# Weight 0 in two parts, the output weight in two halves, and one cast moved to GpSimd

## The chip, the cores and the metric

The kernel runs on one core of a Trainium2 chip. The core has a matrix engine (TensorE, PE in the profile, with its weight loads shown apart as PEld), a vector engine (VectorE, DVE), a scalar engine (ScalarE, ACT), a general engine (GpSimd, POOL) and an engine that mostly issues transfers (SyncE, SP). Transfers between the chip's memory and the core run on 16 DMA engines. Here SP issues the loads of q, k and v, and POOL issues the loads of the weights, which are turned from float32 into bfloat16 on the way. The metric is the time of one execution on the device in microseconds (us), lower is better.

## The reference

Attention with a sliding window of 128 positions and 4 sink positions, over 4 batches, 8 heads, 768 positions and 64 elements a head; then a feed-forward layer that takes the maximum of three products.

```python
scores = scale * q @ k.T                     # per batch and head, 768 x 768
keep   = (key < 4) | ((0 <= query - key) & (query - key < 128))
a      = softmax(where(keep, scores, -1e9))
x      = (a @ v)  -> [3072, 512]             # the 8 heads side by side
h      = max(x @ w1, x @ w2, x @ w3)         # each w is [512, 768]
out    = h @ w_out                           # w_out is [768, 512]
```

The text calls w1, w2 and w3 weight 0, 1 and 2, and w_out the output weight.

## The kernel before

The 3072 positions are cut into 12 chunks of 256 positions, three to a batch. A chunk is loaded as q, k and v of all 8 heads (512 KB each in float32), cast to bfloat16, and q and k are transposed so that the head's elements lie along the partitions. For each of four pairs of heads `score` multiplies keys and queries on PE, `expo` takes the exponential on ACT, `mask` or a mask added beforehand by `premask` cuts the window, `av` multiplies with v on PE, and DVE divides by the sum (a reciprocal and a multiplication, L353 and L356) and writes x. `xpose` transposes x on PE. Then `ffn_h(chunk, third, weight)` multiplies x with 256 of the 768 columns of one weight (eight matmuls, L388); the result for weight 0 is copied by ACT, those for weights 1 and 2 are merged by DVE with a maximum. `ffn_y(chunk, half)` multiplies h with the output weight, six matmuls, one for each block of 128 rows of it (L409).

Nothing reorders the work: each engine runs its instructions in the order in which the program text gives them. For chunks 0 to 2 that order is written out by hand, call by call; from chunk 3 on a loop gives it. Buffers in PSUM are handed out from a list of eight banks, in order of release. Every engine has its own queue, so an instruction that waits holds up all that stand behind it on its engine, issues of transfers among them.

The places that the change and the prediction touch:

- `load_w` (L234) issues a load of some columns of a weight from POOL (L237). In the order by hand weight 0 is loaded whole, weight 1 as columns 512 to 768 and then 0 to 512, weight 2 as three parts of 256 columns.
- `load_wo` (L242) issues the load of the output weight from POOL (L243).
- `cast_v` (L104) casts one half of the positions' parity and one half of the partitions of a chunk's v (L105): four calls to a chunk, each 64 partitions by 512 elements. For chunk 1 three calls go to POOL and one to DVE.
- `cast_qk` (L95) casts half of the heads of q or k (L101). `turn` and `turn2` (L109, L129) transpose such a half on PE (L115, L137) and copy it out of PSUM.
- `after(weight, column)` (L432) gates a load: POOL copies one element of that weight into the tile that the load is going to fill (L435), so the load on SP can only start once the column has arrived. The k of chunk 2 has the gate `after(0, 300)`; the rest of its k, and its q, stand behind it on SP.
- The first `ffn_h` in the order is `ffn_h(0, 2, 0)`: chunk 0, columns 512 to 768, weight 0. The next ones are `ffn_h(0, 0, 0)`, `ffn_h(0, 2, 1)` and `ffn_h(0, 1, 0)`.
- `sink_k` copies the sink keys on POOL (L228); `factors` makes a mask on POOL (L210).

The order around the first edits, with what lies between left out:

```python
        load_w(0, 0, 768)
...
        sink_k(0)
...
        load_w(1, 512, 768)
...
        cast_qk(1, 'q', 1, nc.gpsimd)
        load_w(1, 0, 512)
...
        cast_v(1, 0, 0, nc.gpsimd)
        cast_v(1, 1, 1, nc.gpsimd)
        cast_v(1, 1, 0, nc.gpsimd)
...
        cast_v(1, 0, 1, nc.vector)
        load(2, 'k', part=0, parts=2, gate=after(0, 300))
```

Of the kernel before, what the change touches and what calls it, by code (L numbers as in the profile page):

```python
# [16 lines left out]
def kernel(  # L17
# [13 lines left out]
    nc = tc.nc  # L31
# [13 lines left out]
    FB = d_ff // 128  # L45
# [3 lines left out]
    with tc.manual_schedule():  # L49
# [7 lines left out]
        def bank(shape, dtype, name):  # L57
            j = free.pop(0)
            x = psum.tile(shape, dtype, tag=f"b{j}", name=name)
            home[id(x)] = x, j  # L60
            return x
# [14 lines left out]
        def load(ci, what="kqv", gate=None, part=None, parts=1):  # L76
            if ci >= NCH:
                return
            b, c = divmod(ci, CPB)
            t0 = c * 256  # L80
            for w in what:
                src = {"k": k, "q": q, "v": v}[w]
                if (ci, w) not in raws:
                    raws[ci, w] = raw.tile([128, H, 2, D], F32, tag=w + "_raw", name=w + "_raw")
                dst = raws[ci, w]
                if gate is not None:
                    gate(dst[0:1, 0, 0, 0:1])
                n = H // parts
                for g in range(parts) if part is None else (part,):
                    nc.sync.dma_start(  # L90
                        out=dst[:, n * g:n * g + n],
                        in_=src[b, n * g:n * g + n, t0:t0 + 256]
                            .rearrange("h (p i) d -> p h (i d)", i=2))
# [10 lines left out]
        def cast_v(ci, n, i, eng):  # L104
            eng.tensor_copy(  # L105
                vb[ci % RING][64 * i:64 * i + 64, n, :, 0:D],
                raws[ci, "v"][64 * n:64 * n + 64, :, i])
# [126 lines left out]
        def load_w(wi, c0=0, c1=None):  # L234
            c1 = d_ff if c1 is None else c1
            w = (moe_w1, moe_w2, moe_w3)[wi]
            nc.gpsimd.dma_start(out=w_sb[wi][:, :, c0:c1],  # L237
                                in_=w.rearrange("(a p) f -> p a f", p=128)[:, :, c0:c1])

        wo = const.tile([128, FB, d_model], BF16, name="wo")  # L240

        def load_wo():  # L242
            nc.gpsimd.dma_start(out=wo, in_=moe_w_out.rearrange("(a p) f -> p a f", p=128))  # L243

        es = {}

# [2 lines left out]
        def premask(ci, pairs):  # L249
            lo = 0 if ci % CPB else 1  # L250
            for p in pairs:
                sts[ci, p] = [bank([128, 4, 128], F32, "st") for a in range(2)]
                for a in range(2):
                    nc.tensor.matmul(sts[ci, p][a][:, lo:], lhsT=ident, rhs=addm0 if lo else addm,
                                     start=True, stop=False, skip_group_check=True)

        def score(ci, pairs):
            b, c = divmod(ci, CPB)
            kc, qc = kT[ci % RING], qT[ci % RING]
            lo = 0 if c else 1  # L260
            for p in pairs:
                add = (ci, p) in sts
                if not add:
                    sts[ci, p] = [bank([128, 4, 128], F32, "st") for a in range(2)]
                st = sts[ci, p]
                for s, x, n, q0, q1 in ((0, kT[(ci - 1) % RING], 1, 0, 1), (1, kc, 0, 0, 2),
                                        (3, kc, 1, 1, 2)):
                    if s < lo:
                        continue
                    for a in range(2):  # L270
                        hp = slice(64 * a, 64 * a + 64)
                        nc.tensor.matmul(  # L272
                            st[a][:, s:s + q1 - q0].rearrange("q n (i r) -> q n i r", i=2),
                            lhsT=x[hp, n, p].rearrange("q i r -> q (i r)"),
                            rhs=qc[hp, p, :, q0:q1].rearrange("q i n r -> q n i r"),
                            start=not add, stop=True, skip_group_check=add)
                e = work.tile([128, 2, 4, 128], BF16, tag="e", bufs=2 * NP, name="e_sb")
                es[ci, p] = e, st
# [58 lines left out]
        def av(ci, p):  # L337
            b, c = divmod(ci, CPB)
            o = os_[ci, p]
            e = es[ci, p][0]  # L340
            first = c == 0
            for t in range(2):
                for a in range(2):
                    blocks = [(1, ci, 0)] if t == 0 else [(2, ci, 0), (3, ci, 1)]
                    if t == 0 and c:
                        blocks = [(0, ci - 1, 1)] + blocks
                    for s, cv, n in blocks:
                        nc.tensor.matmul(  # L348
                            o[:, t, a], lhsT=e[:, a, s], rhs=vb[cv % RING][:, n, 2 * p + a],
                            start=first, stop=True, skip_group_check=True)  # L350
                        first = False
            rc = work.tile([128, 2, 2], F32, tag="rc", bufs=4, name="rc")
            nc.vector.reciprocal(rc, o[:, :, :, D])  # L353
            if p == 0:
                xs[ci] = work.tile([128, 2, NP, 2, D], BF16, tag="x", bufs=2, name="x_sb")
            nc.vector.tensor_mul(xs[ci][:, :, p], o[:, :, :, 0:D],  # L356
                                 rc.unsqueeze(3).to_broadcast([128, 2, 2, D]))
            give(o)
# [73 lines left out]
        def after(wi, c=0):  # L432

            def gate(dst):
                nc.gpsimd.tensor_copy(dst, w_sb[wi][0:1, 0, c:c + 1])  # L435
            return gate
# [42 lines left out]
        cast_qk(1, 'k', 0, nc.vector)  # L479
        premask(0, (1,))  # L480
        load(1, 'q')
        load_w(0, 0, 768)
        score(0, (1,))
        score(0, (2,))
        expo(0, 0)
# [21 lines left out]
        cast_v(1, 0, 0, nc.gpsimd)  # L507
        cast_v(1, 1, 1, nc.gpsimd)
        cast_v(1, 1, 0, nc.gpsimd)
        premask(1, (0,))  # L510
        av(0, 3)
        cast_v(1, 0, 1, nc.vector)
        load(2, 'k', part=0, parts=2, gate=after(0, 300))
        score(1, (0,))
        score(1, (2,))
# [36 lines left out]
        ffn_h(1, 0, 0)  # L552
        ffn_h(0, 0, 1)
        load_wo()
        factors(msk0, addm0)
        ffn_h(1, 2, 0)
# [256 lines left out]
```

## Time and profile before

| what | us |
| --- | --- |
| median of 3 runs | 178.63 (178.45 to 179.25) |
| the profiled execution | 178.46 |
| its span in the profile | 176.7 |
| PE busy in the span | 170.9 |
| DVE, ACT, POOL busy | 121.3, 86.1, 64.3 |

The profile is of one execution. Its span begins with the first instruction and ends with the last; the time of the execution is longer by what lies around it. In a timeline's row stand the start and the duration in us, the engine, the line of the kernel, the operation, what it writes and reads, the shape and the number of instructions merged into the row; in brackets stands how long the engine was idle before it and what ended that. A row `q0 software_dynamic` or `q1 hardware_dynamic` gives a DMA queue's packets, megabytes and share of the 16 DMA engines in a window: q0 is the queue of the transfers issued by POOL, q1 that of SP. In the chain of work that ended last, a row is the start, the length and what the end of the span waited for in that stretch.

### The profile page before, as it was taken

The page shows a single profiled execution, that of the slowest core. Times are in us where ns is not written, and L with a number is a line of the kernel's source. Part 1 is how long each engine was busy: PE and PEld are TensorE (multiplying, and loading weights), DVE is VectorE, ACT ScalarE, POOL GpSimd, SP SyncE. Part 2 cuts the span into 40 slices and gives each one's busy share as a digit, 9 for nine tenths or more (in the row PEclk, how much of TensorE's full clock was granted, in tenths as well). Part 3 has the DMA queues.
Part 4 walks back from the last instruction along what each step waited for, and adds up shares of the span by engine and source line. Part 5 has one row for each costly group of instructions (what it writes and reads, how often), then busy time and mean ns, then how long its engine had stood idle before and what let it go on. Part 6 is the DMA issues. An engine that isn't in the chain of part 4 may idle for free.

```text
span 176.7 us, 4647 instructions
## 1 busy us (share of the span) xinstructions
PE 170.9 (97%) x1877; PEld 127.4 (72%) x1877; DVE 121.3 (69%) x263; ACT 86.1 (49%) x172; POOL 64.3 (36%) x123
## 2 busy tenths in 40 slices
PE   7899999999999999999999999999999999999992
PEld 2565899866687687597696696696795795796871
DVE  3388564797698795786785884875785775976451
ACT  4298445768853913923724814814616616420210
POOL 7594505543395593183072145154243000000000
PEclk9999999999999999999999999999999999999999
DMA  5999999999999999997998999999999319203203
GB/s 154 297 284 207 204 220 249 199 293 282 286 228 264 303 205 232 256 201 195 259 202 218 239 193 247 259 162 241 273 165 246 33 25 158 119 4 59 121 0 119
DMA packets 69093, 34.90 MB, mean 198 GB/s; under 512 B 26576, under 2 KB 67536, under 8 KB 69072
## 3 DMA queue, kind: packets, MB, share of 16 engines
q1 hardware_dynamic: 64976, 31.33, 81.1%
q0 software_dynamic: 3952, 3.15, 11.5%
q8 instruction: 14, 0.23, 0.5%
q10 hardware_dynamic: 144, 0.13, 0.2%
q14 instruction: 7, 0.06, 0.1%
HBM read 25.17 MB, written 6.29 MB: 178 GB/s over the span
## 4 chain that ended last, share of the span: by engine, by line
PE 86%; DMA 8%; POOL 1%; DVE 1%; issue 0%; ACT 0%; POOLq 0%; SPq 0%
PE h_ps L388 53%; PE y_ps L409 18%; PE st L272 6%; PE o L348 6%; DMA w<-in_moe_w_dram 5%; DMA v_raw<-in_v_dram 3%; PE pt L115 1%; PE o L330 1%; PE xt L369 1%; PE y_ps L419 1%; PE sk L298 1%; DVE e_sb L290 1%; DVE h_sb L399 0%; ACT h_sb L395 0%; POOL vb L105 0%
## 5 line engine op out<-in xcount | busy, mean ns | idle before, releaser
L388 PE MATMUL h_ps<-xT,w 128*128 128x256 bf16 x864 | 101.4, 273 | 0.3 <-DMA w<-in_moe_w_dram 0.2
L388 PEld LDWEIGHTS <-w 128*128 128x128 bf16 x864 | 82.1, 98 | 10.6 <-issue 0.4
L399 DVE TENSOR_TENSOR h_sb<-h_sb,h_ps 128x512 bf16<-128x512 bf16 (+1 forms) x74 | 49.2, 670 | 21.2 <-PE h_ps L388 19.6
L284 ACT ACTIVATE e_sb<-st 128x512 bf16<-128x512 f32 (+1 forms) x96 | 46.6, 578 | 7.6 <-PE st L272 7.6
L395 ACT CAST h_sb<-h_ps 128x512 bf16<-128x512 f32 x36 | 21.0, 585 | 47.3 <-PE h_ps L388 47.1
L105 POOL CAST vb<-v_raw 64x512 bf16<-64x512 f32 x43 | 28.5, 662 | 18.5 <-DMA v_raw<-in_v_dram 15.8
L409 PE MATMUL y_ps<-wo,h_sb 128*128 128x512 bf16 x138 | 32.5, 380 | 0.0
L290 DVE TENSOR_TENSOR e_sb<-e_sb,msk 128x1024 bf16<-128x1024 bf16 (+1 forms) x41 | 27.1, 698 | 0.9 <-ACT e_sb L284 0.8
L101 POOL CAST k_bf<-k_raw 128x512 bf16<-128x512 f32 x18 | 11.7, 670 | 40.4 <-DMA k_raw<-in_k_dram 33.8
L409 PEld LDWEIGHTS <-h_sb 128*128 128x128 bf16 x138 | 12.4, 98 | 14.4 <-issue 1.6
L356 DVE TENSOR_TENSOR x_sb<-o,rc 128x256 bf16<-128x256 f32 x48 | 20.4, 425 | 1.7
L411 DVE COPY y_sb<-y_ps 128x512 f32<-128x512 f32 x13 | 9.0, 692 | 14.2 <-PE y_ps L409 14.1
L348 PE MATMUL o<-vb,e_sb 128*128 128x65 bf16 x352 | 17.0, 194 | 0.0
L348 PEld LDWEIGHTS <-e_sb 128*128 128x128 bf16 x352 | 14.7, 98 | 2.4 <-issue 0.5
L272 PE MATMUL st<-qT,kT 64*128 64x128 bf16 (+1 forms) x256 | 14.4, 238 | 0.5 <-DVE qT L119 0.5
L272 PEld LDWEIGHTS <-kT 64*128 64x128 bf16 x256 | 8.4, 94 | 7.6 <-issue 5.7
L101 POOL CAST q_bf<-q_raw 128x512 bf16<-128x512 f32 x17 | 10.2, 623 | 6.4 <-DMA q_raw<-in_q_dram 6.4
L353 DVE RECIPROCAL rc<-o 128x4 f32<-128x4 f32 x48 | 8.5, 177 | 4.7 <-PE o L348 4.5
L304 ACT ACTIVATE e_sink<-sk 128x256 bf16<-128x256 f32 x8 | 3.1, 384 | 14.8 <-PE sk L298 14.8
L177 PE MATMUL warm<-wz 128*128 128x512 bf16 x17 | 6.2, 535 | 1.2 <-DVE wz L166 1.2
L411 ACT COPY y_sb<-y_ps 128x512 f32<-128x512 f32 x10 | 5.8, 585 | 3.1 <-PE y_ps L409 2.9
L177 PEld LDWEIGHTS <-wz 128*128 128x128 bf16 x17 | 2.0, 130 | 4.5 <-issue 3.1
(66 smaller groups left out, 72.2 us busy)
## 6 DMA issues: line engine op xcount, KB each, us to landing
k_raw<-in_k_dram SPq DMA_DIRECT2D x11, 512.0 KB, 5.0
v_raw<-in_v_dram SPq DMA_DIRECT2D x11, 512.0 KB, 7.4
out_dram<-y_sb SPq DMA_DIRECT2D x11, 512.0 KB, 3.3
q_raw<-in_q_dram SPq DMA_DIRECT2D x10, 512.0 KB, 7.1
q_raw<-in_q_dram SPq DMA_DIRECT2D x4, 256.0 KB, 6.8
w<-in_moe_w_dram POOLq DMA_DIRECT2D x4, 256.0 KB, 8.7
w<-in_moe_w_dram POOLq DMA_DIRECT2D x1, 768.0 KB, 9.4
wo<-in_moe_w_out_dram POOLq DMA_DIRECT2D x1, 768.0 KB, 10.8
```

The costliest lines, as they stand in the source:

```text
L101: f(x[:, 2 * g:2 * g + 2].rearrange("q p i a d -> q p a i d"), y[:, 4 * g:4 * g + 4].rearrange("q (p a) i d -> q p a i d", a=2))
L105: eng.tensor_copy(vb[ci % RING][64 * i:64 * i + 64, n, :, 0:D], raws[ci, "v"][64 * n:64 * n + 64, :, i])
L272: nc.tensor.matmul(st[a][:, s:s + q1 - q0].rearrange("q n (i r) -> q n i r", i=2), lhsT=x[hp, n, p].rearrange("q i r -> q (i r)"), rhs=qc[ ...
L284: nc.scalar.activation(e[:, a, lo:], st[a][:, lo:], AF.Exp, scale=scale)
L290: (eng or nc.vector).tensor_mul(e[:, :, lo:], e[:, :, lo:], msk0 if lo else msk)
L348: nc.tensor.matmul(o[:, t, a], lhsT=e[:, a, s], rhs=vb[cv % RING][:, n, 2 * p + a], start=first, stop=True, skip_group_check=True)
L356: nc.vector.tensor_mul(xs[ci][:, :, p], o[:, :, :, 0:D], rc.unsqueeze(3).to_broadcast([128, 2, 2, D]))
L388: nc.tensor.matmul(hp[:, f].rearrange("q (i t r) -> q i t r", i=2, t=2), lhsT=w_sb[wi][:, ds, c0:c0 + 128], rhs=xTs[ci][:, :, ds].rearrang ...
L395: nc.scalar.copy(dst, hp)
L399: nc.vector.tensor_max(dst[:, x], dst[:, x], hp[:, x])
L409: nc.tensor.matmul(yp, lhsT=hs[ci][:, fb, t * 128:(t + 1) * 128], rhs=wo[:, fb], start=(fb == 0), stop=(fb == FB - 1))
L411: (nc.scalar.copy if eng is None else eng.tensor_copy)(ys[ci][:, t], yp)
```

## The change

Three edits. Weight 0, loaded by one transfer, is loaded by two: first columns 512 to 768, then columns 0 to 512. The output weight, loaded by one transfer, is loaded by two of three blocks of 128 rows each. Of the four casts of v of chunk 1 the one on DVE goes to POOL, directly behind the other three. On every other engine the instructions and their order stay as they were; POOL has two more transfers to issue and one cast more, DVE one cast less.

```diff
         def load_wo():
-            nc.gpsimd.dma_start(out=wo, in_=moe_w_out.rearrange("(a p) f -> p a f", p=128))
+            x = moe_w_out.rearrange("(a p) f -> p a f", p=128)
+            for a in range(0, FB, FB // 2):
+                nc.gpsimd.dma_start(out=wo[:, a:a + FB // 2], in_=x[:, a:a + FB // 2])
...
         load(1, 'q')
-        load_w(0, 0, 768)
+        load_w(0, 512, 768)
+        load_w(0, 0, 512)
         score(0, (1,))
...
         cast_v(1, 1, 0, nc.gpsimd)
+        cast_v(1, 0, 1, nc.gpsimd)
         premask(1, (0,))
         av(0, 3)
-        cast_v(1, 0, 1, nc.vector)
         load(2, 'k', part=0, parts=2, gate=after(0, 300))
```

## The prediction

> **What bounds the kernel now.** I read the page's busy times, then the chain that ended last, then a table by stage, and only then the timelines of the stage that the change touches.
>
> ```profile
> PE 170.9 (97%) x1877; PEld 127.4 (72%) x1877; DVE 121.3 (69%) x263; ACT 86.1 (49%) x172; POOL 64.3 (36%) x123
> PE 86%; DMA 8%; POOL 1%; DVE 1%; issue 0%; ACT 0%; POOLq 0%; SPq 0%
> 8.98 9.38 DMA w<-in_moe_w_dram
> 8.00:18.40 10.40, 9.33 (x132) 5.40 (x130) 8.27 (x22) 8.93 (x20) 6.45 (x10) 1.00 1.23 246
> 18.40:31.80 13.40, 13.40 (x152) 12.21 (x153) 7.44 (x17) 6.34 (x12) 5.01 (x11) 1.00 1.21 223
> 31.80:42.00 10.20, 10.20 (x130) 7.40 (x128) 8.72 (x16) 7.03 (x14) 5.36 (x10) 1.00 1.18 261
> 52.00:160.00 108.00, 108.00 (x1234) 82.31 (x1232) 79.37 (x168) 50.94 (x103) 36.44 (x63) 1.00 0.94 194
> ```
>
> The third row is the one long transfer in the chain: weight 0, 9.38 us from 8.98. The stage rows give the stretch, its length, PE's busy time, then PEld, DVE, ACT, POOL, the granted clock, the DMA share and GB/s. From 18.40 to 42.00 and again from 52 to 160 PE has no idle time, at a granted clock of 1.00. What the change can win lies in 8.00 to 18.40, where PE is busy 9.33 of 10.40: 1.07 us at the very most. What it can lose lies wherever a later transfer makes PE wait. The DMA share there is 1.18 to 1.23 (packets overlap, so more than 1): the transfers are a second full resource beside PE.
>
> **Weight 0 in two parts, columns 512 to 768 first.** These are the columns that the first `ffn_h` uses.
>
> ```profile
> 17.75 0.42 PE L348 MATMUL o<-vb,e_sb 128*128 128x65 bf16 x8
> 18.40 1.05 PE L388 MATMUL h_ps<-xT,w 128*128 128x256 bf16 x8 [0.23 <-DMA w<-in_moe_w_dram]
> 20.01 2.78 PE L388 MATMUL h_ps<-xT,w 128*128 128x256 bf16 x24
> 18.41 0.18 POOL L435 CAST k_raw<-w 1x1 f32<-1x1 bf16 x1 [2.67 <-DMA w<-in_moe_w_dram]
> q0 software_dynamic: 384, 0.59, 115.7%
> q0 software_dynamic: 186, 0.10, 145.2%
> q0 software_dynamic: 207, 0.21, 125.3%
> ```
>
> PE is done at 17.75 + 0.42 = 18.17 and waits 0.23 for the weight. The last three rows are POOL's DMA queue in 13.2 to 16, 17 to 17.5 and 19 to 20 us: packets, MB, share of the 16 engines. By size per packet (0.59 MB / 384 is 1536 B) the first is weight 0 whole; the other two are mostly pieces 256 and 512 columns wide. Each piece has one packet for each of 512 rows (768 KB / 1536 B). So 512 packets take 512 / 384 x 2.8 = 3.73 us whole, and 512 / 186 x 0.5 = 1.38 and 512 / 207 = 2.47 us in pieces: 3.85, that is 0.12 more. The first piece is there about 2.5 us before the second, near 16.0, so the 0.23 goes. The second lands near 18.4 + 0.1. PE first uses it in the `ffn_h` at 20.01, so even a PE 0.6 earlier does not wait for it.
>
> **POOL's queue, and the cast moved to it.**
>
> ```profile
> 8.98 1.10 POOL L237 DMA_DIRECT2D w<-in_moe_w_dram  x1
> 10.13 0.91 POOL L228 COPY ks<-kT 64x16 bf16<-64x16 bf16 x2
> 10.98 0.74 POOL L237 DMA_DIRECT2D w<-in_moe_w_dram  x1
> 12.00 0.61 POOL L101 CAST q_bf<-q_raw 128x512 bf16<-128x512 f32 x1 [0.28 <-DMA q_raw<-in_q_dram]
> 12.55 0.74 POOL L237 DMA_DIRECT2D w<-in_moe_w_dram  x1
> 13.70 2.04 POOL L105 CAST vb<-v_raw 64x512 bf16<-64x512 f32 x3 [0.40 <-DMA v_raw<-in_v_dram]
> L105 POOL CAST vb<-v_raw x3: 609/616/713, 13.7 to 15.0; 64x512 bf16<-64x512 f32 x3
> 12.67 0.40 PE L115 MATMUL pt<-ident,q_bf 128*128 128x128 bf16 x4
> 14.62 0.65 DVE L105 CAST vb<-v_raw 64x512 bf16<-64x512 f32 x1
> 15.30 0.18 DVE L353 RECIPROCAL rc<-o 128x4 f32<-128x4 f32 x1
> 15.52 0.42 DVE L356 TENSOR_TENSOR x_sb<-o,rc 128x256 bf16<-128x256 f32 x1
> 14.46 0.36 PE L348 MATMUL o<-vb,e_sb 128*128 128x65 bf16 x6
> 16.00 0.51 PE L369 MATMUL xt<-ident,x_sb 128*128 128x128 bf16 x6 [0.20 <-DVE x_sb L356]
> ```
>
> Weight 1's two parts, of the same two widths, are issued in 0.74 each, so two take 1.48 for 1.10: +0.38; if the first issue of the kernel stays at 1.10, +0.74. Behind them on POOL stand the copies of the sink keys, the issue of weight 1's first part and the cast of q at 12.00, which had 0.28 of waiting to give: it starts 0.10 to 0.46 later. PE's transposes of that q follow its end within 0.06 (12.61 to 12.67), so they and all behind them on PE shift by as much.
>
> Against that, DVE loses its cast of 0.65 at 14.62. The reciprocal at 15.30 stood behind it; its matmuls ended at 14.46 + 0.36 = 14.82, so with the same 0.06 it can start at 14.88, and x is ready 0.64 later, at 15.52 instead of 15.94. With the shift of 0.10 to 0.46 that is 15.62 to 15.98, so PE's transposes at 16.00 come 0.32 earlier to no earlier at all. The first `ffn_h` follows: from 18.40 to 18.17 - 0.32 = 17.85, or to 18.2, a gain of 0.55 to 0.20 at that place. I take 0.5, since 0.74 is what both widths cost elsewhere.
>
> The fourth cast on POOL, at the longest of the three (0.71), ends at 13.70 + 2.04 + 0.71 = 16.45, or 16.9 with the shift. Its user is `av(1, 0)` at 17.75, 17.4 with PE's gain: hidden. After it POOL waited 2.67 for weight 0 anyway, so the added POOL time reaches no later issue. Without that cover it would go onto the gate one for one.
>
> **What hangs on the second piece.** The gate `after(0, 300)` at 18.41 reads column 300, which is now in the second piece.
>
> ```profile
> 18.53 0.74 POOL L237 DMA_DIRECT2D w<-in_moe_w_dram  x1
> 18.61 0.92 SPq L90 DMA_DIRECT2D k_raw<-in_k_dram  x2
> 19.64 1.01 SPq L90 DMA_DIRECT2D q_raw<-in_q_dram  x2
> 31.04 0.43 DVE L101 CAST q_bf<-q_raw 128x512 bf16<-128x512 f32 x1 [0.52 <-DMA q_raw<-in_q_dram]
> 30.73 1.04 PE L388 MATMUL h_ps<-xT,w 128*128 128x256 bf16 x8
> 31.61 0.39 PE L115 MATMUL pt<-ident,q_bf 128*128 128x128 bf16 x4
> ```
>
> Behind that gate stand, on POOL, the three issues of weight 2, and on SP the loads of k and q of chunk 2. The last part of that q lands at 31.04 (DVE waited 0.52 for it), its cast ends at 31.47, and PE, which comes straight from the `ffn_h` of 30.73, transposes it at 31.61. With 0.06 from the cast to PE, 0.08 us are to spare. This is the step that decides: PE works in order, so whatever it gains before 31.61 it spends waiting for this q, unless the q comes earlier too. With queues full throughout (share 1.21), 0.12 us more of packets ahead puts the q 0.12 later: 0.12 - 0.08 = +0.04 us for PE. The bounds: the data of weight 0 can start earlier by the shorter issue at most, 1.10 to 0.74, so -0.36 for the q, and then PE gains 0.36 + 0.08 = 0.44; and later by one more issue of 0.74, so 0.74 - 0.08 = +0.66. I take +0.04: the count of packets is the nearest row, and as the engines are full before and behind, an earlier start only pushes back what they did instead (v of chunk 1).
>
> **Output weight in two halves.**
>
> ```profile
> 26.95 0.82 POOL L243 DMA_DIRECT2D wo<-in_moe_w_out_dram  x1
> 27.85 1.08 POOL L210 TENSOR_SCALAR msk<-addm 128x384 bf16<-128x384 bf16 x2
> 32.85 1.26 POOL L105 CAST vb<-v_raw 64x512 bf16<-64x512 f32 x2 [3.93 <-DMA v_raw<-in_v_dram]
> wo<-in_moe_w_out_dram POOLq DMA_DIRECT2D x1, 768.0 KB, 10.8
> 37.94 1.47 PE L409 MATMUL y_ps<-wo,h_sb 128*128 128x512 bf16 x6
> ```
>
> It lands at 26.95 + 10.8 = 37.75 and is used at 37.94, so the whole had 0.19 to spare; a PE that were earlier by more than that would wait here next. In halves the packets stay as they are (same rows), the first three of six matmuls need the first half only, and the second half is due three matmuls, about 0.7 us (half of 1.47), later. So even 0.5 us late it costs nothing. The second issue (between 0 and 0.82 more; 0.74 taken) falls into the 3.93 that POOL waits at 32.85. Price 0; it is cover for the other edits.
>
> **The sum.** Before 31.6 PE gains 0.5 and gives it back waiting for q of chunk 2; that wait ends 0.04 later than PE came before. Behind it PE has no idle time to absorb or give. The profiled execution took 178.46 us (span 176.7), 0.17 below the median of 178.63: 178.46 + 0.04 = 178.5.
>
> **Rivals.**
>
> *The gain comes through.* The q of chunk 2 lands half a microsecond earlier, because the second piece, and with it the gate, does. Then all 0.55 stays: 177.9. For it: the issue is shorter. Against it: the engines are full, and packets only get more. More than 0.89 us (0.5%) would need nearly all of the 1.07 us that PE idles before 18.40.
>
> *The gate comes late (slower).* The gate hangs on a piece that is now second in the queue. If that piece has to pay a start of its own, everything behind the gate moves. The price from the trace: weight 0 was issued by 8.98 + 1.10 = 10.08, and from 11.9 to 13.1 the queue shows only its first 45 packets:
>
> ```profile
> q0 software_dynamic: 45, 0.07, 31.6%
> ```
>
> so a start costs 1.8 to 3.0 us; the time would be 178.46 + 1.8 - 0.08 = 180.2 up to 181.4. It counts as slower from a gate 0.97 late (0.89 + 0.08). Against it: in all three stretches shown between 13.2 and 20 the queue, with three DMAs one behind the other, keeps its share at 116 to 145%.
>
> The Trainium skill (page "DMA: Bandwidth & Descriptors", section "Anatomy of one DMA — SWDGE (gpsimd) path") gives each DMA a fixed cost of about 2.0 us beside its bytes, which speaks for few large ones and against this split. Paid one behind the other, that would put the gate 2.0 us later and the time at an estimated 180.4. The full shares above say that such costs overlap in this queue, so the rule shares the small chance of this rival.
>
> *The change does not do what it says.* The first issue stays at 1.10, POOL's cast of q comes 0.46 late, PE's early work slips by as much, and the first `ffn_h` starts only 0.2 earlier. As PE waits for q of chunk 2 anyway, the end is the same: 178.5.
>
> **How the numbers follow.** Measurement of this kernel tells about 0.5% (0.89 us) from no change. Likeliest case 0.70: 178.5, its own bounds 178.46 - 0.44 = 178.0 to 178.46 + 0.66 = 179.1. The issue staying long, 0.10, the same time. The gain coming through, 0.10, of which 0.04 for more than 0.89. The late gate, 0.10. So faster 0.04; slower 0.10 and 0.02 of the likeliest case, for a q later than its bound, 0.12; within 0.5% 0.84. The range is 177.9, the first rival, to 179.2, just above the upper bound; it leaves out the late gate and the strong form of the first rival, under 2 in 10.
>
> **What the changed profile would show.** First `ffn_h` at 17.8 to 18.2 with no wait for a weight (else the piece came late). POOL: two issues of 0.74 from 8.98, four casts of v in a row. DVE: no cast near 14.6, x ready near 15.6. POOL's gate on weight 0 at 18.4 to 18.6. Then the mark of the argument: PE idle some half a microsecond before the transposes of q near 31.6, behind a cast on DVE that waited for q. If they start by 31.2 with no wait, the first rival holds; if the gate stands past 19.4, the second. PE should not wait for the output weight near 38. The prediction is wrong if a wait appears that no case here has, above all from 31.8 on.

## The result and the profile after

| | median us | lowest to highest | executions |
| --- | --- | --- | --- |
| before | 178.91 | 178.32 to 179.46 | 22 |
| changed | 178.34 | 177.75 to 181.50 | 22 |

The ratio of changed to before is 0.9974, interval 0.9961 to 0.9986: about 0.26% or 0.47 us faster. The execution of 181.50 is a slow one and is left out of the ratio. The gain is within the 0.5% that the prediction called no change, and it lies at 0.9974 x 178.46 = 178.0 on the scale of the predicted sum, which said 178.5. The time is within the range, but it came about in another way than the likeliest case: it is near that of the first rival, "the gain comes through" (177.9). It also lies at the lower edge of what the likeliest case allowed (178.0 to 179.1), but there for an earlier gate, and the gate came later. As far as the mechanism goes, it is luck that the range holds the time. The profiled execution took 178.04 us, its span 176.3.

First the page's busy times, shares of the chain of work, and the table by stage of the changed kernel (the columns are those of the prediction: stretch, length, PE, PEld, DVE, ACT, POOL, granted clock, DMA share, GB/s).

```profile
PE 169.8 (96%) x1864; PEld 127.0 (72%) x1877; DVE 120.7 (68%) x262; ACT 86.0 (49%) x172; POOL 66.4 (38%) x126
PE 88%; DMA 3%; POOL 3%; DVE 2%; issue 2%; POOLq 0%; SPq 0%; DVEq 0%
8.00:18.40 10.40, 9.62 (x134) 5.59 (x135) 7.79 (x22) 8.76 (x21) 7.38 (x12) 1.00 1.28 244
18.40:31.80 13.40, 13.40 (x154) 12.22 (x152) 7.77 (x18) 6.38 (x13) 5.68 (x12) 1.00 1.23 230
31.80:42.00 10.20, 10.15 (x133) 7.38 (x132) 8.51 (x18) 7.10 (x15) 5.27 (x11) 1.00 1.17 264
52.00:160.00 108.00, 107.58 (x1223) 82.16 (x1230) 79.25 (x168) 50.84 (x102) 36.63 (x63) 1.00 0.94 195
```

From 8.00 to 18.40 PE is busy 9.62 us instead of 9.33 (granted clock 1.00 in both). From 18.40 to 31.80 it has no idle time, as before: the idle half microsecond that the prediction expected ahead of 31.6 is not there. The timeline shows the same step by step; first PE, then DVE, then POOL.

```profile
12.88 0.40 PE L115 MATMUL pt<-ident,q_bf 128*128 128x128 bf16 x4
17.59 0.42 PE L350 MATMUL o<-vb,e_sb 128*128 128x65 bf16 x8
17.85 1.03 PE L390 MATMUL h_ps<-xT,w 128*128 128x256 bf16 x8
30.17 1.04 PE L390 MATMUL h_ps<-xT,w 128*128 128x256 bf16 x8
31.04 0.39 PE L115 MATMUL pt<-ident,q_bf 128*128 128x128 bf16 x4
37.38 1.47 PE L411 MATMUL y_ps<-wo,h_sb 128*128 128x512 bf16 x5
15.29 0.42 DVE L358 TENSOR_TENSOR x_sb<-o,rc 128x256 bf16<-128x256 f32 x1
30.48 0.43 DVE L101 CAST q_bf<-q_raw 128x512 bf16<-128x512 f32 x1 [0.52 <-DMA q_raw<-in_q_dram]
9.23 1.71 POOL L237 DMA_DIRECT2D w<-in_moe_w_dram  x2
12.22 0.61 POOL L101 CAST q_bf<-q_raw 128x512 bf16<-128x512 f32 x1
13.76 2.58 POOL L105 CAST vb<-v_raw 64x512 bf16<-64x512 f32 x4 [0.25 <-DMA v_raw<-in_v_dram]
18.68 0.18 POOL L437 CAST k_raw<-w 1x1 f32<-1x1 bf16 x1 [2.34 <-DMA w<-in_moe_w_dram]
```

x is ready at 15.29 + 0.42 = 15.71 (15.94 before), and the first `ffn_h` starts at 17.85 without a wait (18.40). The transposes of q of chunk 2 start at 31.04 (31.61) and the output weight's matmuls at 37.38 (37.94): the 0.55 us pass both places where they could be lost. The q that was to hold PE back was there at 30.48, not at 31.16, although the gate on weight 0 came later than before (18.68 against 18.41). Of the 0.56 us at the output weight, 0.41 are left at the sink scores of chunk 4, where PE came at 55.56 before. The first two rows are of the kernel before, the others of the changed one:

```profile
55.56 0.28 PE L298 MATMUL sk<-qT,ks 128*32 128x256 bf16 x4
171.78 1.47 PE L419 MATMUL y_ps<-wo,h_sb 128*128 128x256 bf16 x12
```

```profile
55.15 0.28 PE L300 MATMUL sk<-qT,ks 128*32 128x256 bf16 x4
171.37 1.47 PE L421 MATMUL y_ps<-wo,h_sb 128*128 128x256 bf16 x12
```

With 0.41 less the last matmuls start too (171.37 against 171.78), and the execution ends 0.42 sooner (178.04 against 178.46). So all of the difference is made before 55 us, and behind that nothing is gained or lost: from the sink scores to the last matmuls both take 116.22 us. The 107.58 busy of 108.00 after 52 us is therefore no idle time, but some ten matmul records that the trace lacks (1223 instead of 1234).

### The profile page after: what moved, and what is told of

Read it like the earlier page. It is cut to its first block, busy times and chain, and to the rows that moved or that the text cites. A ratio compares the mean times of both kernels' runs of the same rounds, so it can differ in the third digit from the quotient of the medians.

```text
span 176.3 us, 4635 instructions
## 1 busy us (share of the span) xinstructions
PE 169.8 (96%) x1864; PEld 127.0 (72%) x1877; DVE 120.7 (68%) x262; ACT 86.0 (49%) x172; POOL 66.4 (38%) x126
## 3 DMA queue, kind: packets, MB, share of 16 engines
q0 software_dynamic: 4496, 3.15, 11.7%
## 4 chain that ended last, share of the span: by engine, by line
PE 88%; DMA 3%; POOL 3%; DVE 2%; issue 2%; POOLq 0%; SPq 0%; DVEq 0%
PE h_ps L390 52%; PE y_ps L411 17%; PE st L274 6%; PE o L350 6%; DMA v_raw<-in_v_dram 3%; PE pt L115 1%; PE xt L371 1%; DVE h_sb L401 1%; PE o L332 1%; PE sk L300 1%; PE st L256 1%; POOL w L237 1%; PE y_ps L421 1%; DVE e_sb L292 1%; POOL vb L105 0%
## 5 line engine op out<-in xcount | busy, mean ns | idle before, releaser
L390 PEld LDWEIGHTS <-w 128*128 128x128 bf16 x864 | 82.0, 98 | 10.3 <-issue 0.4
L105 POOL CAST vb<-v_raw 64x512 bf16<-64x512 f32 x44 | 29.6, 673 | 16.1 <-DMA v_raw<-in_v_dram 11.3
L411 PE MATMUL y_ps<-wo,h_sb 128*128 128x512 bf16 x126 | 31.9, 380 | 0.6
L358 DVE TENSOR_TENSOR x_sb<-o,rc 128x256 bf16<-128x256 f32 x48 | 20.4, 425 | 1.7
L177 PE MATMUL warm<-wz 128*128 128x512 bf16 x16 | 5.6, 501 | 1.3 <-DVE wz L166 1.2
L237 POOL DMA_DIRECT2D w<-in_moe_w_dram x7 | 5.4, 773 | 0.0
```

Of the source, the lines that this page charges most:

```text
L105: eng.tensor_copy(vb[ci % RING][64 * i:64 * i + 64, n, :, 0:D], raws[ci, "v"][64 * n:64 * n + 64, :, i])
L358: nc.vector.tensor_mul(xs[ci][:, :, p], o[:, :, :, 0:D], rc.unsqueeze(3).to_broadcast([128, 2, 2, D]))
L390: nc.tensor.matmul(hp[:, f].rearrange("q (i t r) -> q i t r", i=2, t=2), lhsT=w_sb[wi][:, ds, c0:c0 + 128], rhs=xTs[ci][:, :, ds].rearrang ...
L411: nc.tensor.matmul(yp, lhsT=hs[ci][:, fb, t * 128:(t + 1) * 128], rhs=wo[:, fb], start=(fb == 0), stop=(fb == FB - 1))
```

## The experiments

The experiments come in three groups, each on a chip of its own with its own runs of the kernel before. The ratios are against these, with their intervals. All kernels compute the whole of the reference.

The first four go for the deciding step: is it q of chunk 2 that swallows the gain?

### Weight 0 in two parts alone

```diff
-        load_w(0, 0, 768)
+        load_w(0, 512, 768)
+        load_w(0, 0, 512)
```

> Only weight 0 in two parts; the cast of v stays on DVE and the output weight is whole. Both theories: the first ffn_h no longer waits for its weight, but x is as late as before or 0.2 us later (POOL's cast of q comes later), so it starts at 18.1 to 18.4 instead of 18.40. Theory 'first h' (the end moves with the start of the first ffn_h): 0.0 to -0.3 us. Theory 'q of chunk 2' (the end moves with the landing of that q, 31.0 before and 30.4 in the changed kernel): if the two pieces are what brings the q in earlier, it lands near 30.4 here too and PE, not the q, is late; the same 0.0 to -0.3 us. If it lands at 31.0 or later, no gain at all.

Measured: ratio 1.0010 (0.9991 to 1.0029), median 178.97 against 178.61.

### The cast on GpSimd alone

```diff
         cast_v(1, 1, 0, nc.gpsimd)
+        cast_v(1, 0, 1, nc.gpsimd)
...
-        cast_v(1, 0, 1, nc.vector)
```

> Only the cast of v moved to GpSimd. x is ready 0.43 us earlier (15.5 instead of 15.94), but weight 0 is whole and lands at 18.4 as before, so the first ffn_h starts at 18.4. Both theories: within 0.1 us of before. A gain of 0.3 us or more would say that neither is right and that DVE's time after 18.4 counts.

Measured: ratio 1.0009 (0.9985 to 1.0033), median 178.84.

### Both, the output weight whole

The two diffs above together; `load_wo` as before.

> Weight 0 in two parts and the cast moved, output weight whole. First ffn_h near 17.85 as in the changed kernel. Theory 'first h': -0.45 us, less what PE waits for the whole output weight near 37.4 (landing 37.2 to 37.8, so 0 to 0.4 us). Theory 'q of chunk 2' as the prediction had it (landing moves only with the count of packets): 0.0 us, with PE idle some 0.5 us before the transposes of that q.

Measured: ratio 1.0023 (1.0002 to 1.0045), median 179.24.

### The kernel before once more

No edit, a single execution with its profile: how far do two profiles of one kernel lie apart?

> The kernel before once more, for a second profile. If the landing of the last part of q of chunk 2 is steady, it is at 31.0 within 0.1 us and its cast on DVE starts at 31.04; if it scatters by 0.3 us or more between executions, the 0.6 us between the two profiles at that place isn't due to the change.

Measured: 179.22 us, span 177.4 (178.46 and 176.7 in the profile of before).

What these four show. PE's early work starts at other times in every execution (its transposes of q of chunk 1 anywhere from 12.67 to 13.71), so I count from these transposes to the first `ffn_h`. The rows of PE's timeline, in the order weight alone, cast alone, both, before once more:

```profile
13.09 0.39 PE L115 MATMUL pt<-ident,q_bf 128*128 128x128 bf16 x4
18.74 1.03 PE L388 MATMUL h_ps<-xT,w 128*128 128x256 bf16 x8
```

```profile
13.08 0.39 PE L115 MATMUL pt<-ident,q_bf 128*128 128x128 bf16 x4
18.59 1.05 PE L388 MATMUL h_ps<-xT,w 128*128 128x256 bf16 x8 [0.38 <-DMA w<-in_moe_w_dram]
```

```profile
13.07 0.39 PE L115 MATMUL pt<-ident,q_bf 128*128 128x128 bf16 x4
18.04 1.04 PE L388 MATMUL h_ps<-xT,w 128*128 128x256 bf16 x8
```

```profile
13.61 0.40 PE L115 MATMUL pt<-ident,q_bf 128*128 128x128 bf16 x4
18.89 0.93 PE L388 MATMUL h_ps<-xT,w 128*128 128x256 bf16 x7
```

The distance is 5.65 with the weight alone, 5.51 with the cast alone, 4.97 with both, and 5.28 and 5.73 in the two profiles of before. In all fourteen profiles it is 4.96 to 4.98 where both edits are in (seven profiles) and 5.28 to 5.73 where one or both are missing (seven). So at this place the two early edits work only together. With the cast alone PE is early and waits 0.38 for the weight that is still whole; with the weight alone the weight is there, but x comes no earlier, since DVE casts ahead of it (x is ready 3.58 us behind the transposes, 3.27 before). Together they are worth 0.3 to 0.8 us from the transposes to the first `ffn_h`. The prediction's 0.55 holds there.

The cast of q of chunk 2 on DVE, in the same order:

```profile
30.77 0.42 DVE L101 CAST q_bf<-q_raw 128x512 bf16<-128x512 f32 x1
```

```profile
30.63 0.42 DVE L101 CAST q_bf<-q_raw 128x512 bf16<-128x512 f32 x1
```

```profile
30.20 0.43 DVE L101 CAST q_bf<-q_raw 128x512 bf16<-128x512 f32 x1
```

```profile
30.92 0.42 DVE L101 CAST q_bf<-q_raw 128x512 bf16<-128x512 f32 x1
18.10 0.50 POOL L435 CAST k_raw<-w 1x1 f32<-1x1 bf16 x1 [1.48 <-DMA w<-in_moe_w_dram]
```

None of these casts waited for a transfer: q was there earlier still. In the first profile it was waited for until 31.04. So 31.04 was one execution's value. And yet both edits together, the output weight whole, were not faster. What they gain was lost, and not to this q.

### The changed kernel once more

No edit against the changed kernel; it is the scale for the next three, on the second chip.

> The changed kernel once more, beside the same runs of the kernel before as the next three. Ratio near 0.997 if the first comparison holds on another chip; 1.000 or more if what was measured there belongs to the chip. In its profile the first ffn_h starts 0.3 to 0.6 us earlier, counted from the same point of PE's work at 12 us, than in the kernel before, without a wait for weight 0; the last part of q of chunk 2 lands at 30.2 to 30.5, as it did in five of the six profiles so far, and PE doesn't wait for it.

Measured: ratio 0.9963 (0.9949 to 0.9977), median 178.10 (177.97 to 178.35) against 178.75.

### Both early edits and the output weight whole, once more

```diff
-            x = moe_w_out.rearrange("(a p) f -> p a f", p=128)
-            for a in range(0, FB, FB // 2):
-                nc.gpsimd.dma_start(out=wo[:, a:a + FB // 2], in_=x[:, a:a + FB // 2])
+            nc.gpsimd.dma_start(out=wo, in_=moe_w_out.rearrange("(a p) f -> p a f", p=128))
```

(against the changed kernel)

> Weight 0 in two parts and the cast moved, output weight whole, again, now beside the changed kernel on one chip. If the halves of the output weight do nothing (they have no wait to remove: in the profile of the first such run PE started on the output weight at 37.57 without a wait), the time is within 0.2 us of the changed kernel. If the 1.0023 of the first run was due to the whole output weight, it is 0.5 us or more slower than the changed kernel.

Measured: ratio 0.9997 (0.9971 to 1.0023), median 178.87. On the same chip the changed kernel has 178.10, its slowest execution 178.35, and eleven of these twelve are slower than that. So with both early edits in place, the halves are worth 0.77 us there. The twelve executions fall into two groups, 178.33 to 178.69 and 179.04 to 179.63, six in each. The profiled one took 179.04; its rows of PE at the output weight and its list of transfers say why:

```profile
37.18 0.29 PE L330 MATMUL o<-vs,e_sink 32*128 32x130 bf16 x8
38.63 1.47 PE L409 MATMUL y_ps<-wo,h_sb 128*128 128x512 bf16 x6 [1.16 <-DMA wo<-in_moe_w_out_dram]
wo<-in_moe_w_out_dram POOLq DMA_DIRECT2D x1, 768.0 KB, 11.8
```

PE was on time (its first `ffn_h` at 17.88) and stood 1.16 us for the output weight, which took 11.8 us from issue to landing instead of 10.8. Over the six profiles with the whole output weight in its old place it took 10.3 to 11.8 us, and it landed between 36.9 and 38.6; PE needs it at about 37.9 in the kernel before and at 37.4 once it is half a microsecond early. In halves (seven profiles, 8.1 to 8.9 us a half in the median) no profile shows PE waiting for it. This is a wait in one execution of the kernel; that it is the cause of the slower six is argued from that row, not counted in each of them. It is also not all that the halves save: in the five other profiles the whole weight landed 0.2 to 1.1 us ahead of its first use, and the faster six (178.33 to 178.69) are still some 0.4 us slower than the changed kernel.

### The second part of weight 0 issued later

```diff
         load_w(0, 512, 768)
-        load_w(0, 0, 512)
...
         sink_k(0)
+        load_w(0, 0, 512)
```

(against the changed kernel)

> The changed kernel with the second part of weight 0 issued behind the copies of the sink keys. The same POOL work, so POOL's cast of q of chunk 1 does not start earlier by the count (0.0 us). Should the copies of the sink keys run in the shadow of another wait, 0.1 to 0.2 us of the 0.2 that PE loses at 12.7 come back. The gate on weight 0 stays within 0.2 us, since the first part keeps the queue busy until 14. Both theories: within 0.2 us of the changed kernel.

Measured: ratio 0.9976 (0.9955 to 0.9997), median 178.28: no better. The first `ffn_h` stays 4.97 behind the transposes (13.55 to 18.52), so the order of issues there is not what sets the gain.

### The gate on k of chunk 2 a microsecond later

```diff
-        load(2, 'k', part=0, parts=2, gate=after(0, 300))
+        load(2, 'k', part=0, parts=2, gate=after(1, 600))
```

(against the changed kernel)

> The changed kernel, but k of chunk 2 is gated by the first part of weight 1 instead of the second part of weight 0: the gate opens 1.0 us later (19.7 instead of 18.7), and with it the loads of k and q of chunk 2 and the issues of weight 2. Theory 'q of chunk 2 sets the end': its last part lands 1.0 us later and PE waits for it near 31, the time is 0.6 to 1.0 us longer than the changed kernel's. Theory 'the queues have room there': the landing moves by 0.4 us or less, PE waits 0 to 0.3 us, and the time stays within 0.3 us.

Measured: ratio 0.9979 (0.9961 to 0.9997), median 178.42. From POOL's, DVE's and PE's timelines:

```profile
19.69 0.18 POOL L437 CAST k_raw<-w 1x1 f32<-1x1 bf16 x1 [2.56 <-DMA w<-in_moe_w_dram]
31.10 0.43 DVE L101 CAST q_bf<-q_raw 128x512 bf16<-128x512 f32 x1 [0.32 <-DMA q_raw<-in_q_dram]
31.87 0.39 PE L115 MATMUL pt<-ident,q_bf 128*128 128x128 bf16 x4
```

The gate is 1.01 later than in the changed kernel's first profile and 2.18 later than in its second (17.51, below). But PE is late in this execution as well: its transposes of q of chunk 1 start at 13.71, against 12.88 and 12.99. Counted from these, the gate is only 0.18 and 1.46 later. The q comes 0.62 and 0.35 later, and its cast ends 0.34 ahead of this late PE (31.87 less 31.10 + 0.43). The median is 178.42 against 178.10 on the same chip. The intervals overlap, but eight of the twelve executions are slower than the slowest of the changed kernel (178.35). So the later gate costs some 0.3 us: less than "q of chunk 2 sets the end" foretold, and at the edge of what "the queues have room there" did. Where it is lost the profile does not show, since PE does not wait for this q in it.

The third group takes the other combinations.

### The halves alone

```diff
-            nc.gpsimd.dma_start(out=wo, in_=moe_w_out.rearrange("(a p) f -> p a f", p=128))
+            x = moe_w_out.rearrange("(a p) f -> p a f", p=128)
+            for a in range(0, FB, FB // 2):
+                nc.gpsimd.dma_start(out=wo[:, a:a + FB // 2], in_=x[:, a:a + FB // 2])
```

> Only the output weight in two halves. Theory 'late output weight' (a whole output weight lands at 36.9 to 38.6 from execution to execution, and PE, which needs it near 37.9 here, waits for it in some of them): PE's first use doesn't wait in any, so the median comes down by 0.1 to 0.3 us, ratio 0.998 to 0.9995. Theory 'the halves do nothing by themselves' (they cover only the 0.5 us that the other two edits win): ratio 1.000, within 0.1 us.

Measured: ratio 0.9999 (0.9985 to 1.0014), median 178.45 against 178.50.

### The halves and the cast

The changed kernel with weight 0 whole.

> The cast moved and the output weight in halves, weight 0 whole. The first ffn_h waits for weight 0 (18.4 to 18.6), so the cast brings nothing: like the halves alone, within 0.1 us. If instead it is like the changed kernel (ratio near 0.996), weight 0 in two parts does nothing.

Measured: ratio 0.9999 (0.9986 to 1.0012), median 178.62.

### The halves and weight 0 in two parts

The changed kernel with the fourth cast of v on DVE.

> Weight 0 in two parts and the output weight in halves, the cast left on DVE. x comes as late as before or later (POOL's cast of q is 0.2 us later), so the first ffn_h starts no more than 0.1 us earlier: like the halves alone within 0.15 us. If it is like the changed kernel, the cast does nothing.

Measured: ratio 0.9983 (0.9967 to 1.0000), median 178.31.

With these, all eight combinations are measured (ratio to before; where there are two, from two groups):

```
                     output weight whole     output weight in halves
neither              1                       0.9999
weight 0 split       1.0010                  0.9983
cast on GpSimd       1.0009                  0.9999
both                 1.0023 and 0.9997       0.9974 and 0.9963
```

Only with all three does an interval lie clear of 1 on the fast side. The early edits without the halves give nothing, the halves alone give nothing, together they give 0.26 to 0.37%. The halves with the split alone come near it: their interval ends at 1.0000 and overlaps both of the full change. That the cast is needed too is shown at the first `ffn_h`, and not by these times.

### The output weight issued earlier

In place of the halves: both early edits, the output weight whole, and its issue moved ahead of a cast of k that waits on POOL.

```diff
         av_open(1)
+        load_wo()
         cast_qk(2, 'k', 1, nc.gpsimd)
...
         ffn_h(0, 0, 1)
-        load_wo()
         factors(msk0, addm0)
```

> Weight 0 in two parts, the cast moved, the output weight whole but issued right behind weight 2, ahead of the cast of k of chunk 2 on which POOL waits 5 us: at 21 instead of 27. Its packets can follow weight 2's at once, from 28 on. Theory 'late output weight': it lands before 37.3 and PE doesn't wait for it, so the time is that of the changed kernel within 0.2 us (ratio 0.995 to 0.9975), though it is whole; the price would be q of chunk 2 or 3 coming later. Theory 'something else in the halves' (two transfers, their later end): ratio 0.999 or more, as the other two runs with a whole output weight had.

Measured: ratio 1.0055 (1.0034 to 1.0075), median 179.45 of seven executions: slower. DVE's and PE's timelines, the list of waits and the list of transfers:

```profile
31.43 0.43 DVE L101 CAST q_bf<-q_raw 128x512 bf16<-128x512 f32 x1 [1.36 <-DMA q_raw<-in_q_dram]
31.91 0.40 PE L115 MATMUL pt<-ident,q_bf 128*128 128x128 bf16 x4 [0.60 <-DVE q_bf L101]
PE o L348 <- DVE e_sb L290: 0.5, 1, 0.5
wo<-in_moe_w_out_dram POOLq DMA_DIRECT2D x1, 768.0 KB, 14.3
```

Here the prediction's deciding step does happen. The output weight, issued at 21.01, lands at 35.3, and PE does not wait for it. But its packets run beside q of chunk 2, the q comes at 31.43, and PE waits 0.60 for its cast, and 0.5 for another result of DVE near 42. The mechanism is real; in the changed kernel's two profiles it costs nothing and 0.1 us. The test does not settle what the halves do, since this order brings waits of its own.

No kernel that was run beats the changed one.

### All fourteen profiles side by side

PE's time up to the sink scores of chunk 4 can be cut at three common points: T is the start of its transposes of q of chunk 1, A runs from there to the first `ffn_h`, B on to the first matmul with the output weight, C on to the sink scores at some 55 us. In twelve of the fourteen the execution's time is the sum plus 122.9 (plus 123.1 in the first profile of both early edits, 123.2 in the one with the later issue).

```
                                       T      A      B      C     sum    time
whole    before                      12.67   5.73  19.54  17.62  55.56  178.46
         before once more            13.61   5.28  19.53  17.90  56.32  179.22
         weight 0 split              13.09   5.65  19.53  17.84  56.11  179.03
         cast                        13.08   5.51  19.54  18.01  56.14  179.04
         both                        13.07   4.97  19.53  18.12  55.69  178.81
         both, once more             12.91   4.97  20.75  17.52  56.15  179.04
         both, issued earlier        12.98   4.98  20.30  18.29  56.55  179.45
halves   neither                     13.14   5.31  19.53  17.34  55.32  178.24
         cast                        12.75   5.65  19.54  17.75  55.69  178.59
         weight 0 split              13.21   5.56  19.53  17.35  55.65  178.54
         changed                     12.88   4.97  19.53  17.77  55.15  178.04
         changed, once more          12.99   4.96  19.63  17.54  55.12  178.01
         changed, issue later        13.55   4.97  19.53  17.56  55.61  178.81
         changed, gate later         13.71   4.97  19.52  17.85  56.05  178.97
```

T scatters by a microsecond whatever the kernel. Most of that is there before the edits act: T follows POOL's cast of a part of chunk 0's v, for whose load POOL waits. It starts at 8.42 in the profile of before and at 9.27 in that of the later gate:

```profile
8.42 0.61 POOL L105 CAST vb<-v_raw 64x512 bf16<-64x512 f32 x1 [1.29 <-DMA v_raw<-in_v_dram]
```

```profile
9.27 0.84 POOL L105 CAST vb<-v_raw 64x512 bf16<-64x512 f32 x1 [1.29 <-DMA v_raw<-in_v_dram]
```

Counted from that start, T also holds a price of the split, which A leaves out. T comes 4.25 or 4.26 us behind it in four of the five profiles with weight 0 whole (4.59 with the cast alone), and 4.36 to 4.75 behind it in the nine with the split: 0.1 to 0.5 us more, as the prediction had it. From this cast to the first `ffn_h` the seven profiles with both early edits take 9.32 to 9.72 us, and the three with neither 9.54 to 9.98. The means are 0.23 apart, so the net gain is less than A alone shows.

A is the work of the two early edits: 4.96 to 4.98 against a mean of 5.53. B is rigid at 19.53 but for the waits named above (1.2 for the output weight, 0.8 for q where the output weight was issued earlier, 0.1 for q in the changed kernel's second profile). C was not in the prediction at all, and it scatters by 0.8 us, from 17.34 to 18.12 (18.29 with the wait for the mask in the kernel that issues the output weight earlier). In the first profile of both early edits with the whole weight, where PE met no wait in B, C is 0.50 longer than in the first profile of before (18.12 against 17.62), of a gain of 0.76 in A (5.73 to 4.97). Of these 0.50, 0.32 is one wait just ahead of the sink scores, shown under "What stays open". Two more causes of C can be seen. One is k of chunk 3: ACT casts it late, and the copy of its transposes, which PE waits for before the first scores near 43.8, comes late with it. From the first matmul with the output weight to these scores it is 5.85 us without that wait. It was 5.98 to 6.14 in four of the five profiles with the whole weight in its place and no wait in B, 5.85 to 5.87 in six of the seven with halves, and 5.95 with the late gate. So in these profiles the wait for k is mostly gone with the halves. The cast of that k started at 40.44 to 41.37 in the six profiles with the whole output weight in its place and at 39.93 to 40.37 in six of the seven with halves (41.04 with the late gate). The longest case is the kernel with the cast alone, in ACT's timeline and in the waits:

```profile
41.16 0.62 ACT L101 CAST k_bf<-k_raw 128x512 bf16<-128x512 f32 x1 [0.94 <-DMA k_raw<-in_k_dram]
PE st L272 <- ACT kT L122: 0.2, 1, 0.2
```

The other is a pair of DVE's multiplications with the mask near 49, while POOL casts v. Here it is in the second profile of the changed kernel and in the first:

```profile
48.78 1.43 DVE L292 TENSOR_TENSOR e_sb<-e_sb,msk 128x768 bf16<-128x768 bf16 x2
```

```profile
48.60 1.87 DVE L292 TENSOR_TENSOR e_sb<-e_sb,msk 128x768 bf16<-128x768 bf16 x2
```

It takes 1.43 in three profiles (the halves alone, the halves with the split, the changed kernel once more), and there the sixteen `ffn_h` matmuls ahead of the next `av` take PE 1.75 us; in the other eleven it takes 1.64 to 1.87, and they take 1.93 to 1.97. What decides which of the two it is was not tested.

## Why the prediction was right and wrong

**Where the gain is (right).** The first `ffn_h` was to come at 17.85 to 18.2 and came at 17.85, with the wait for the weight gone and x ready at 15.71 (15.62 to 15.98 foretold). All four casts of v on POOL were hidden, as costed: POOL waited 2.34 us at the gate behind them. One thing was not seen: at this place the gain needs the split and the cast both, and each alone brings nothing. The prediction added a 0.23 and a 0.32 in one sum and did not say that neither is to be had without the other.

**POOL's two issues (mis-sized, within bounds).** 1.71 instead of 1.48; of the two bounds the upper one (1.84) was nearer. POOL's cast of q came at 12.22, 0.22 later, inside 0.10 to 0.46.

**The gate (mis-sized).** 18.68 in place of 18.53: 0.27 later where the count of packets said 0.12. In the second profile of the changed kernel it stands before that of the first profile of before:

```profile
17.51 0.18 POOL L437 CAST k_raw<-w 1x1 f32<-1x1 bf16 x1 [0.98 <-DMA w<-in_moe_w_dram]
30.75 0.43 DVE L101 CAST q_bf<-q_raw 128x512 bf16<-128x512 f32 x1 [0.68 <-DMA q_raw<-in_q_dram]
```

17.51 and 18.68 are one and the same kernel. A term of 0.12 us was worked out for a landing that scatters by 1.2. The rule of the Trainium skill (page "DMA: Bandwidth & Descriptors", section "Anatomy of one DMA — SWDGE (gpsimd) path"), 2.0 us for each DMA beside its bytes, did not show as a delay of the gate. Paid one behind the other, it would have put the gate at an estimated 18.41 + 2.0 = 20.4, and the two profiles have 18.68 and 17.51.

**"This is the step that decides" (the step that failed).** The prediction took q of chunk 2 as fixed at 31.04 + 0.12 and gave the whole gain back there. The landing is not fixed. Where DVE waited for it, so that the landing itself is seen, it came at 30.19, 30.48, 30.75, 31.04, 31.07, 31.10 and 31.43, the last two in kernels that delay it on purpose or crowd it out; in seven profiles it came unseen before 30.20 to 30.92. It does not follow the gate: 17.51 goes with 30.75, 18.68 with 30.48, 18.41 with 31.04. Nor does it follow PE: counted from the first `ffn_h` it came 12.80 behind in the changed kernel's second profile and less than 12.03 behind with the halves alone. A spare time of 0.08 us, read from one execution, was made the turning point of the forecast while that landing moves by 0.9 us between executions. It also took the later end of what it saw. In the changed kernel's two profiles PE lost nothing at this q in the first and about 0.1 us in the second (0.96 us from the `ffn_h` at 30.27 to the transposes at 31.23, where the first profile has 0.87, from 30.17 to 31.04). What sets the landing of q within its 0.9 us was not found.

**"Price 0" for the halves (the second miss).** The words beside it, that the halves are cover for the other edits and that an earlier PE would wait on the output weight next, were right; the sum did not use them. By the prediction PE would not come earlier there, so the cover would be worth nothing. Measured, it is what lets the gain through: 0.9974 and 0.9963 with the halves, 1.0023 and 0.9997 without, 178.10 against 178.87 on one chip. The wait for the output weight is only part of it; the wait for k of chunk 3, which the prediction did not look at, is another. Again the 0.19 us to spare was one execution's: the whole lands between 36.9 and 38.6, from 1.07 ahead of PE to 1.16 too late.

**"Behind it PE has no idle time to absorb or give" (the third miss).** The stage table of the prediction went from 42.00 straight to 52. C, which ends near 55.7 and has its waits in that gap and behind it, scatters by 0.8 us; the changed kernel's first profile lost 0.15 of its 0.56 us there.

**The rivals.** "The gain comes through" is what happened, though not by its mechanism: it had the gate come earlier, and what was seen is a q whose landing did not follow the gate. "The gate comes late" fell, since the gate moved by 0.27. Where it was moved on purpose, the kernel lost 0.3 us, and PE did not wait for this q. But PE was itself late there: at the 31.04 of the changed kernel's first profile it would have waited some half a microsecond for a cast that ends at 31.53. So the mechanism of that rival is not refuted. "The change does not do what it says" fell with the `ffn_h` at 17.85.

**What stays open.** How the gain of the halves divides between the wait for the output weight itself (B) and what lands behind it (C) is not settled, nor why k of chunk 3 lands earlier with them. The mean of C is 17.90 in the five profiles with the whole weight in its place and no wait for it, and 17.59 in the seven with halves, but single profiles scatter by more than these 0.31, and the halves alone are not faster (0.9999). Both early edits with the whole output weight were 0.23% slower than before on the first chip, where a lost gain explains no more than equal. The profile of that run has the longest C but one and shows one more wait, ahead of the sink scores of chunk 4: from the `av` behind the sixteen `ffn_h` matmuls to these scores it takes 3.47 us, and 3.15 or 3.16 in the other thirteen. The timeline's place and the list of waits for 54 to 72 us:

```profile
55.69 0.29 PE L298 MATMUL sk<-qT,ks 128*32 128x256 bf16 x4
PEld L298 <- DMA qT<-q_bf: 0.4, 1, 0.4
```

On the second chip the same kernel was level with before. Whether the whole output weight makes this wait more frequent wasn't tried.

## What to carry to other kernels

A margin of 0.1 to 0.2 us at a transfer's landing, read from one profile while the queues are full, is not a margin and not a wait: here such landings moved by 0.9 us (q), 1.2 us (weight 0) and 1.7 us (the output weight) between executions, so give such a step a chance and not a value. When work ahead of a chain of landings is made earlier, list the transfers that come next on it and make room at each, for the edits may be worth something only together: of eight combinations here only the full one was clearly faster than before. And compare two profiles by stretches between common points of the code, not by the clock from the start of the span.

## What the runs showed of the hardware

The length of one and the same stretch of early work differs between executions by more than the change is worth. The first matmuls, fourteen of equal shape that run ahead of the data, took 4.51 us in one execution and 5.92 in another, with identical code up to there; the first lines are of the kernel with both early edits and the whole output weight, second run, the others of the kernel before once more. The second line of each is the source line's summary: minimum, median and maximum of one matmul in ns, with the first and last start.

```profile
1.20 4.51 PE L177 MATMUL warm<-wz 128*128 128x512 bf16 x14 [1.20 <-DVE wz L166]
L177 PE MATMUL warm<-wz x17: 378/381/635, 1.2 to 10.2; 128*128 128x512 bf16 x17
```

```profile
1.20 5.92 PE L177 MATMUL warm<-wz 128*128 128x512 bf16 x14 [1.20 <-DVE wz L166]
L177 PE MATMUL warm<-wz x16: 379/634/634, 1.2 to 11.1; 128*128 128x512 bf16 x16
```

Most of them took 381 ns in the one and 634 in the other, while the granted clock of 0 to 8 us reads 1.00 in both. The Trainium skill (page "TensorE: Matmul & The Clock Gate", section "🔬 Part 1: The HAM clock gate (the "warmup" mystery)") has a matmul of this width start every 426.7 ns while the array is cold and every 215.7 ns once warm, and the change come after about 3.4 us of work. The trace agrees in kind: two durations of one shape, 253 ns apart. How many matmuls take the longer time differs between executions of the same code, and the clock's column doesn't show it. This lag is not what moves T: these matmuls took 5.08 us in the profile with the latest T (13.71) and 6.06 in one with a T of 13.21.

The other surprise is how little a second transfer of the same bytes costs this queue: weight 0 in two parts put the gate 0.27 later in one profile and 0.90 earlier in the other. Over all profiles with this gate it opens at 17.66 to 18.60 with weight 0 whole (five) and at 17.51 to 18.84 with the two parts (eight). The issue of both parts took POOL 1.71 us, 0.61 more than the whole.
